# Down products of three late blocks from reduced-precision parts, with two accumulator banks per block

## The chip, the cores and the metric

The kernel runs on one core of a Trainium2 chip. The metric is the device time of one execution in microseconds (us), and the time of the kernel before is the median of three runs. The profile is one execution taken by the hardware profiler; its span runs from the first to the last instruction and is a little shorter than the device time.

## The reference

An attention with polynomial sketches, followed by a SwiGLU feed-forward. Only the second half matters here.

```python
# attention: q, k, v of shape (4, 4, 1088, 32); its output becomes x of shape (4352, 128)
g = x @ w_gate                        # (4352, 1536)
silu = g * (1.0 / (1.0 + np.exp(-g)))
val = x @ w_val                       # (4352, 1536)
return (silu * val @ w_out).astype(np.float32)   # (4352, 128)
```

Inputs are float32, and the products have to come out at about float32 precision.

## The kernel before, in words

All data is held transposed: features on the 128 partitions, tokens along the free dimension. The 1536 hidden features are 12 chunks of 128 (`NCH`), so the weights are `wg[:, j, :]`, `wv[:, j, :]` and `wo[:, j, :]` for chunk j. The tokens of the first batch are three small blocks. Those of the other three batches are seven blocks, the list `line`: six of 480 tokens and a last one of 384. A "unit" is one chunk of one block, and the main loop runs over `y` from 0 to 83, with block `line[y // 12]` and chunk `y % 12`. So units 36 to 47 are the fourth block of the line, 48 to 59 the fifth and 60 to 71 the sixth.

TensorE does a float32 product in two ways. The plain way (one call, two records in the trace) takes float32 operands. The other way cuts each operand into parts of a shorter type, float32r, and gets the same sum from three products. With `w1` the upper part of w, `w0` the rest, `wb` = BETA * w0, `wd` = w1 - BETA * w0, and likewise `x1`, `x0`, `xd` = x1 - BETA * x0, BETA = 4096:

- the "difference product" d = wd . xd is read by ScalarE and scaled by -1/BETA;
- the "sum product" p = w1 . x1 + wb . x0 is read by VectorE, scaled by 1 + 1/BETA and added to it.

The gate and value products of a late unit (`cut_unit` with `both`, from unit 20 on) are made in this way, in this order on each engine:

- TensorE: two difference products (L902), into one pair of PSUM banks, then four part products of the sum (L910, L911), into another pair.
- ScalarE: the copy of the differences, 960 elements wide (L906). Then `finish()` ends the unit before: its Silu (L918).
- VectorE: the combine (L912), 960 wide, from PSUM and the copy.
- GpSimd: hidden = silu * value (L923), also in `finish()`, so one unit later.
- TensorE: `down()`, a plain product (L976) with `wo`, for the hidden chunk of six units before. It accumulates the 12 chunks of a block in one PSUM bank, and after the last one `store` transposes it on VectorE (L1005) and sends it out.

Each engine works through its instructions in the order in which the program issues them; there is no other planner. PSUM has eight banks. In the late units `g2` and `acc` are held for the accumulators of the down products, and the other six are three pairs. `pair()` takes them in turn, and a unit uses two. So the differences of unit y + 2 go where the sums of unit y were, once VectorE has combined them, and the sums of unit y + 1 go where the differences of unit y were, once ScalarE has copied them.

Down products are due when more than five hidden chunks wait, and the loop may issue two in a unit. One line makes the first product of `line[1]` wait a unit longer, as its bank has just been used:

```python
if len(todo) > min(5 + (todo[0] == (line[1], 0)), END - y + 1):
    down()
```

The tokens of the next block are cut into `x1`, `x0`, `xd` nine units before it starts (ScalarE L873, then GpSimd L874) and four units before it (VectorE L878). For the fifth to seventh block of the line that is at the end of units 40 and 44, 51 and 56, 63 and 68. At the start of unit 40 the last group of the attention, `numerators(3)`, also runs.

Of the kernel before, what the change touches and what calls it, by code (L numbers as in the profile page):

```python
# [19 lines left out]
def kernel(  # L20
# [104 lines left out]
    def pair():  # L125

        i = min((i for i in (0, 4, 6) if i not in held), key=lambda i: max(used[i], used[i + 1]))
        touch(i, i + 1)
        return PS[:, i : i + 2, :]
# [13 lines left out]
    wg = const.tile([P, NCH, P], FP32, name="wg")  # L143
    wv = const.tile([P, NCH, P], FP32, name="wv")
    wo = const.tile([P, NCH, D], FP32, name="wo")
    kld = const.tile([P, 4 * NC, Dh], FP32, name="kld")
    qld = const.tile([P, 4 * NC, Dh], FP32, name="qld")
    vld = const.tile([P, H, NC, Dh], FP32, name="vld")
    kT = const.tile([P, NC, 4, 32], FP32, name="kT")
    qT = const.tile([P, 4 * NC, 32], FP32, name="qT")  # L150
    raw = {}
    kpieces = ((0, 5), (5, NC))
    fpieces = ((0, 3), (3, 6), (6, NC))
# [147 lines left out]


    NH = 27
    hbuf = const.tile([P, NH, BW], FP32, name="hbuf")
    slots = [hbuf[:, k, :] for k in range(NH)]
    slot_of = {}

    xT = const.tile([P, NT], FP32, name="xT")
# [297 lines left out]
    def attentions():  # L606

        yield from turn_keys(1)  # L610
        yield from turn_queries(1)
        hold("a")
        kp = wide("a")
        for i, c in enumerate(kpieces):
            key_products(kp[:, i, :], *c)
        ka = apool.tile([P, NC * H, R], FP32, tag="kas", name="kas")

        def sketch(ps, i):
            c0, c1 = kpieces[i]
            return ps[:, i, 0 : 64 * (c1 - c0)].rearrange("p (x t r) -> p x t r", t=2, r=R)  # L620

        for i, (c0, c1) in enumerate(kpieces):
            nc.scalar.copy(ka[:, H * c0 : H * c1, :], sketch(kp, i)[:, :, 0, :])
        phk = apool.tile([P, NC, H, R, R], FP32, tag="phk", name="phk")
        for n, (i, c0, c1) in enumerate(((0, 0, 3), (0, 3, 5), (1, 5, 7), (1, 7, 9))):
            first = H * (c0 - kpieces[i][0])
            kb = sketch(kp, i)[:, first : first + H * (c1 - c0), 1, :]
            key_features(phk, (ka[:, H * c0 : H * c1, :], kb), c0, c1)
            if n == 3:
                release("a")  # L630
            if n % 3 != 1:
                yield
        zs, sums = feature_sums(phk)
        for f in sums:
            f()
        yield from turn_keys(2)
        kvz = wide("a")
        values(kvz[:, 0, :], phk, zs)
        kab, kcopies = sketched(wide("b"), key_products, 2, "kab2")
        fold(kvz[:, 0, :])  # L640
        spread = spread_out(1, kvz[:, 0, :])
        hold("a", "b")
        yield
        qab, copies = sketched(wide("a"), query_sketches, 3, "qab")
        run_copies(copies, 2)
        yield
        run_copies(kcopies, 2)
        release("a", "b")
        for n, _ in enumerate(query_step(1, qab)):
            if n % 2 == 1:  # L650
                yield
        yield
        yield
        numerators(1, spread)
        yield "first"

        phk = apool.tile([P, NC, H, R, R], FP32, tag="phk", name="phk")
        yield from features(phk, kab)
        zs, sums = feature_sums(phk)
        for f in sums:  # L660
            f()
        yield from turn_keys(3)
        yield from turn_queries(2)
        for b in (2, 3):
            yield "pe"
            if b == 3:
                numerators(2, spread)
            hold("a")
            kv = bank()
            kv_bank = [max(used, key=used.get)]  # L670
            release("a")
            values(kv, phk, zs)
            if b == 2:
                kab, copies = sketched(wide("a"), key_products, 2, "kab2")
                run_copies(copies, 2)
            fold(kv)
            spread = spread_out(b, kv)
            touch(*kv_bank)
            yield
            yield "pe"  # L680
            qab, copies = sketched(wide("b"), query_sketches, 3, "qab")
            run_copies(copies, 2)
            yield
            if b == 2:
                yield from turn_queries(3)
                phk = hbuf[:, NH - 6 :, :].rearrange("p s (n h i j) -> p (s n) h i j", h=1, i=R, j=R)
                phk = phk.rearrange("p (c h) o i j -> p c (h o) i j", h=H)
                yield from features(phk, kab)
                zs, sums = feature_sums(phk)
            yield from beside(query_step(b, qab), sums)  # L690
        yield "pe"
        numerators(3, spread)
        yield
# [171 lines left out]
    def cut_tokens(i, engine=nc.gpsimd):  # L865
# [14 lines left out]
            op0=ALU.mult, op1=ALU.add,  # L880
        )

    room = [None, 2]

    def doubles(k):
# [4 lines left out]
        room[1] += k  # L890
        return room[0][:, at : at + k, :]

    def cut_unit(i, j, both=False):

        t0, n = blocks[i]
        x1, x0, xd = (x[:, 0:n] for x in x_parts[i])
        ws = (wg, wv) if both else (wv,)
        parts = [[x[:, j % 3, :] for x in w_parts[id(w), j // 3]] for w in ws]
        ds = pair()[:, :, 0:n] if both else bank()[:, 0:n].unsqueeze(1)
        g = None if both else bank()[:, 0:n]  # L900
        for k, (_, _, wd) in enumerate(parts):
            nc.tensor.matmul(ds[:, k], wd, xd, start=True, stop=True)  # L902
        if not both:
            nc.tensor.matmul(g, wg[:, j, :], xT[:, t0 : t0 + n], start=True, stop=True)  # L904
        sums = doubles(len(ws))[:, :, 0:n]
        nc.scalar.activation(sums, ds, AF.Copy, scale=-1.0 / BETA)  # L906
        finish()
        ps = pair()[:, :, 0:n] if both else bank()[:, 0:n].unsqueeze(1)
        for k, (w1, wb, _) in enumerate(parts):
            nc.tensor.matmul(ps[:, k], w1, x1, start=True, stop=False)  # L910
            nc.tensor.matmul(ps[:, k], wb, x0, start=False, stop=True)  # L911
        nc.vector.scalar_tensor_tensor(  # L912
            out=sums, in0=ps, scalar=1.0 + 1.0 / BETA, in1=sums, op0=ALU.mult, op1=ALU.add
        )

        def last():
            sg = fpool.tile([P, WB], FP32, tag="sg", name="sg", bufs=5)[:, 0:n]
            nc.scalar.activation(sg, sums[:, 0] if both else g, AF.Silu)  # L918
            slot_of[i, j] = slots.pop(0)
            hj = slot_of[i, j]  # L920
            hidden[i, j] = hj
            todo.append((i, j))
            nc.gpsimd.tensor_tensor(out=hj[:, 0:n], in0=sg, in1=sums[:, len(ws) - 1], op=ALU.mult)  # L923

        if both:
            ending.append(last)
        else:
            last()
# [4 lines left out]
    def finish():  # L933
        while ending:
            ending.pop(0)()
# [29 lines left out]
        o, sg = lates.pop(0)  # L965
        nc.gpsimd.tensor_tensor(out=o, in0=o, in1=sg, op=ALU.mult)

    line = list(range(HEAD, len(blocks)))

    def down():  # L970

        i, j = todo.pop(0)
        n = SPLIT if i == LAST else blocks[i][1]
        if j == 0:
            acc[i] = bank("g1" if i == 1 else "g2" if i in line[2::2] else "acc")
        nc.tensor.matmul(  # L976
            acc[i][:, 0:n],
            wo[:, j, :],
            hidden[i, j][:, 0:n],
            start=(j == 0),  # L980
            stop=(j == NCH - 1),
        )
        if i != LAST:
            hidden.pop((i, j))
            slots.append(slot_of[i, j])
        if j == NCH - 1:
            store(i, n)

    def straight(ps, j):

# [238 lines left out]
    run(x_steps or cut_tokens(HEAD, nc.vector))  # L1229

    flat = hbuf[:].rearrange("p s w -> p (s w)")
    slots[:] = [flat[:, WB * k : WB * k + WB] for k in range((NH - 10) * BW // WB)]

# [7 lines left out]
            token_steps.setdefault(at, []).append(gen)  # L1243
    oldest[0] = True
    hold("acc")
    lows = [hbuf[:, NH - 10 + c, :].rearrange("p (c f) -> p c f", f=P) for c in range(4)]
    gate_rows = []
    for y in range(END):
        i, j = line[y // NCH], y % NCH
        if y in GROUPS:  # L1250
            group()
        if y == GATES:
            hold("g2")
        if y == END - 1:
            finish()
            unit(i, j)
        else:
            cut_unit(i, j, both=y >= GATES)
        for _ in range(2):

            if len(todo) > min(5 + (todo[0] == (line[1], 0)), END - y + 1):
                down()
        parts_of(y < GATES or y % 2 == 0)
        if y == 0:
            gate_rows = cut_weights(wg, lows, nc.vector)
        for n, row in enumerate(gate_rows):
            if y >= (0, 2, 6, 6)[n]:
                take(row, 1)
        for gen in token_steps.get(y, ()):
            next(gen, None)  # L1270
    ps = wide("a")[:, 0, 0:D]
    for j in range(NCH):
        if todo and j % 4 == 0:
# [40 lines left out]
```

## Time and profile before

| | us |
|---|---|
| device time, median of 3 (287.96 to 288.39) | 288.08 |
| span of the profile | 286.6 |
| TensorE busy, products | 278.4 |
| VectorE busy | 202.7 |
| ScalarE busy | 165.7 |
| GpSimd busy | 156.2 |

In the lines of the profile, PE is TensorE (PEld its weight loads), DVE VectorE, ACT ScalarE, POOL GpSimd. A row of a group has line, engine, operation, names out<-in with their shapes, count, then busy us, mean ns of one, and the idle time of the engine just before it with what ended that. A product's own time is longer than the distance between two starts, as products are pipelined; distances between starts say what TensorE spends on one. The granted clock of TensorE was 1.00 throughout.

### The profile page before, as it was taken

The page shows a single profiled execution, that of the slowest core. Times are in us where ns is not written, and L with a number is a line of the kernel's source. Part 1 is how long each engine was busy: PE and PEld are TensorE (multiplying, and loading weights), DVE is VectorE, ACT ScalarE, POOL GpSimd, SP SyncE. Part 2 cuts the span into 40 slices and gives each one's busy share as a digit, 9 for nine tenths or more (in the row PEclk, how much of TensorE's full clock was granted, in tenths as well). Part 3 has the DMA queues.
Part 4 walks back from the last instruction along what each step waited for, and adds up shares of the span by engine and source line. Part 5 has one row for each costly group of instructions (what it writes and reads, how often), then busy time and mean ns, then how long its engine had stood idle before and what let it go on. Part 6 is the DMA issues. An engine that isn't in the chain of part 4 may idle for free.

```text
span 286.6 us, 5490 instructions
## 1 busy us (share of the span) xinstructions
PE 278.4 (97%) x2117; PEld 188.7 (66%) x2117; DVE 202.7 (71%) x309; ACT 165.7 (58%) x297; POOL 156.2 (55%) x157
## 2 busy tenths in 40 slices
PE   7899999999999999999999999999999999999994
PEld 6545565666665675555676767757767777677884
DVE  3997988975595977999658889646656655675641
ACT  3468665723401857555276776756776767766750
POOL 3315432279500895499745756546657557566560
PEclk9999999999999999999999999999999999999999
DMA  6574193222311133001000020002000100200201
GB/s 194 154 223 110 55 287 115 80 78 80 98 25 27 26 90 82 2 0 27 11 16 0 1 37 0 0 2 34 0 0 15 23 0 0 34 0 2 34 1 28
DMA packets 26137, 14.27 MB, mean 50 GB/s; under 512 B 19840, under 2 KB 24192, under 8 KB 26112
## 3 DMA queue, kind: packets, MB, share of 16 engines
q1 hardware_dynamic: 25456, 13.84, 18.8%
q8 instruction: 16, 0.26, 0.4%
q10 hardware_dynamic: 656, 0.10, 0.2%
q14 instruction: 9, 0.07, 0.1%
HBM read 11.41 MB, written 2.23 MB: 48 GB/s over the span
## 4 chain that ended last, share of the span: by engine, by line
PE 89%; DVE 5%; ACT 2%; DMA 2%; issue 1%; SPq 0%; DVEq 0%; ACTq 0%
PE PS L976 28%; PE PS L945 16%; PE PS L902 11%; PE PS L910 10%; PE PS L911 10%; PE PS L904 5%; PE PS L774 2%; PE PS L333 2%; PE PS L345 2%; DMA kld<-in_k_dram 2%; PE PS L379 1%; DVE sum L912 1%; PE PS L991 1%; PE PS L488 1%; PE PS L436 1%
## 5 line engine op out<-in xcount | busy, mean ns | idle before, releaser
L923 POOL TENSOR_TENSOR hbuf<-sg,sum 128x480 f32<-128x480 f32 (+1 forms) x83 | 103.3, 1249 | 60.2 <-ACT sg L918 52.9
L912 DVE SCALAR_TENSOR_TENSOR sum<-PS,sum 128x960 f32<-128x960 f32 (+2 forms) x83 | 83.5, 1006 | 48.3 <-ACT sum L906 42.5
L906 ACT ACTIVATE sum<-PS 128x960 f32<-128x960 f32 (+2 forms) x83 | 70.9, 854 | 51.0 <-PE PS L902 50.9
L976 PE MATMUL PS<-hbuf,wo 128*128 128x480 f32 (+3 forms) x240 | 100.3, 517 | 0.0
L976 PEld LDWEIGHTS PS<-hbuf,wo 128*128 128x128 f32 x240 | 45.0, 189 | 13.1 <-issue 0.9
L902 PE MATMUL PS<-xd,gphq 128*128 128x480 f32 (+1 forms) x63 | 44.8, 711 | 0.5 <-DVE xd L878 0.5
L910 PE MATMUL PS<-x,w 128*128 128x480 f32 (+1 forms) x83 | 38.6, 465 | 0.0
L918 ACT ACTIVATE sg<-sum 128x480 f32<-128x480 f32 (+1 forms) x63 | 36.5, 580 | 0.6 <-DVE sum L912 0.6
L902 PE MATMUL PS<-xd,wd 128*128 128x480 f32 (+1 forms) x83 | 35.8, 431 | 0.5 <-DVE xd L878 0.5
L911 PE MATMUL PS<-x,wb 128*128 128x480 f32 (+1 forms) x83 | 31.3, 378 | 0.0
L945 PE MATMUL PS<-xT,wg 128*128 128x384 f32 (+1 forms) x74 | 29.5, 480 | 0.0
L945 PE MATMUL PS<-xT,wv 128*128 128x384 f32 (+1 forms) x74 | 28.8, 471 | 0.2 <-DVE wv L279 0.2
L949 ACT ACTIVATE sg<-PS 128x384 f32<-128x384 f32 (+1 forms) x31 | 14.4, 467 | 21.3 <-PE PS L945 19.6
L902 PEld LDWEIGHTS PS<-xd,wd 128*128 128x128 f32 x83 | 15.7, 189 | 15.5 <-issue 14.6
L910 PE MATMUL PS<-x,graw 128*128 128x480 f32 (+1 forms) x63 | 23.6, 374 | 0.2 <-ACT xT L791 0.2
L960 DVE TENSOR_TENSOR hbuf<-sg,PS 128x384 f32<-128x384 f32 (+1 forms) x31 | 16.2, 525 | 10.5 <-PE PS L945 10.1
L911 PE MATMUL PS<-x,graw 128*128 128x480 f32 (+1 forms) x63 | 23.4, 371 | 0.0
L902 PEld LDWEIGHTS PS<-xd,gphq 128*128 128x128 f32 x63 | 11.8, 188 | 13.7 <-issue 11.1
L945 PEld LDWEIGHTS PS<-xT,wv 128*128 128x128 f32 x74 | 13.8, 190 | 9.2 <-DVE hbuf L960 0.9
L910 PEld LDWEIGHTS PS<-x,w 128*128 128x128 f32 x83 | 15.6, 188 | 5.9 <-issue 3.4
L945 PEld LDWEIGHTS PS<-xT,wg 128*128 128x128 f32 x74 | 13.3, 189 | 9.3 <-issue 1.2
L911 PEld LDWEIGHTS PS<-x,wb 128*128 128x128 f32 x83 | 15.6, 188 | 5.8 <-issue 4.3
(131 smaller groups left out, 345.8 us busy)
## 6 DMA issues: line engine op xcount, KB each, us to landing
kld<-in_k_dram SPq DMA_DIRECT2D x4, 544.0 KB, 4.4
vld<-in_v_dram SPq DMA_DIRECT2D x12, 144.0 KB, 4.4
qld<-in_q_dram SPq DMA_DIRECT2D x3, 544.0 KB, 3.5
raw<-in_moe_w_out_dram SPq DMA_DIRECT2D x4, 384.0 KB, 3.8
raw<-in_moe_w_gate_dram SPq DMA_DIRECT2D x3, 384.0 KB, 3.7
raw<-in_moe_w_val_dram SPq DMA_DIRECT2D x3, 384.0 KB, 3.7
out_dram<-o SPq DMA_DIRECT2D x16, 60.0 KB, 2.0
vld<-in_v_dram SPq DMA_DIRECT2D x4, 112.0 KB, 4.4
```

Source lines behind the costliest of these rows:

```text
L902: nc.tensor.matmul(ds[:, k], wd, xd, start=True, stop=True)
L904: nc.tensor.matmul(g, wg[:, j, :], xT[:, t0 : t0 + n], start=True, stop=True)
L906: nc.scalar.activation(sums, ds, AF.Copy, scale=-1.0 / BETA)
L910: nc.tensor.matmul(ps[:, k], w1, x1, start=True, stop=False)
L911: nc.tensor.matmul(ps[:, k], wb, x0, start=False, stop=True)
L912: nc.vector.scalar_tensor_tensor(out=sums, in0=ps, scalar=1.0 + 1.0 / BETA, in1=sums, op0=ALU.mult, op1=ALU.add)
L918: nc.scalar.activation(sg, sums[:, 0] if both else g, AF.Silu)
L923: nc.gpsimd.tensor_tensor(out=hj[:, 0:n], in0=sg, in1=sums[:, len(ws) - 1], op=ALU.mult)
L945: nc.tensor.matmul(o[:, 0:n], w[:, j, :], xT[:, t0 : t0 + n], start=True, stop=True)
L949: nc.scalar.activation(sg[:, 0:n], g[:, 0:n], AF.Silu)
L960: nc.vector.tensor_tensor(out=hj[:, 0:n], in0=sg[:, 0:n], in1=u[:, 0:n], op=ALU.mult)
L976: nc.tensor.matmul(acc[i][:, 0:n], wo[:, j, :], hidden[i, j][:, 0:n], start=(j == 0), stop=(j == NCH - 1),)
```

## The change

In the fourth, fifth and sixth block of the line (`line[3:6]`) the down products of the six odd chunks are made from parts like the others. That is 18 of 84 down products of the line. It needs:

- `cut_down`: parts of the odd chunks of `wo`, made once in nine steps at units 24, 26, ... 40. The even chunks are scaled by -BETA, so that their plain products can go into the differences' bank.
- `cut_hidden`: parts of each odd hidden chunk of unit y: `h1` on ScalarE in unit y + 2 behind the Silu, `h0` on GpSimd in unit y + 3 ahead of that unit's product, `hd` on VectorE in unit y + 4 ahead of that unit's combine.
- two banks per block: `g2` takes the difference products and the scaled plain ones, `acc` the sum products. Before, blocks took `g2` and `acc` in turn.
- `put_together`: in the unit behind a block's last down product ScalarE copies `g2` (behind the Silu), in the next VectorE adds `acc` (`sum2`, ahead of the combine), and in the one after that `store` runs.
- the first down product of the fifth to seventh block waits one unit longer, so one unit has none and the next has two.
- storage: the parts take the place of tiles that are no longer read (`late`, `kld`, `qld`, `vld`, `kT`, `qT`).

```diff
+    DOWN = [(i, j) for i in line[3:6] for j in range(1, NCH, 2)]
+    def cut_down():
+        n = NCH // 2
+        parts = const.tile([P, 3, n, D], F32R, tag="late", name="dparts", bufs=1)
+        w1, wb, wd = (parts[:, k] for k in range(3))
...
+        odd, even = wo[:, 1::2, :], wo[:, 0::2, :]
+        cs = [slice(c, c + 2) for c in range(0, NCH // 2, 2)]
+        nc.scalar.activation(w1, odd, AF.Copy, scale=CUT)
+        yield
+        for c, x in zip(cs, low):
+            nc.gpsimd.tensor_tensor(
+                out=x, in0=odd[:, c], in1=whole(w1[:, c]), op=ALU.subtract
+            )
+            yield
+        for c, x in zip(cs, low):
+            nc.scalar.activation(wb[:, c], x, AF.Copy, scale=BETA)
+        yield
+        for c in cs:
+            nc.gpsimd.tensor_tensor(
+                out=wd[:, c], in0=whole(w1[:, c]), in1=whole(wb[:, c]), op=ALU.subtract
+            )
+            yield
+        nc.scalar.activation(scaled, even, AF.Copy, scale=-BETA)
+    def cut_hidden(y, i, j):
...
+        h_sets.append(h_sets.pop(0))
+        h1, h0, hd = h_parts[i, j] = [x[:, 0:n] for x in h_sets[-1]]
+        h = hidden[i, j][:, 0:n]
+        add_to(behind, y + 2, lambda: nc.scalar.activation(h1, h, AF.Copy, scale=CUT))
+        add_to(before, y + 3, lambda: nc.gpsimd.tensor_tensor(
+            out=h0, in0=h, in1=whole(h1), op=ALU.subtract
+        ))
+        add_to(before, y + 4, lambda: nc.vector.scalar_tensor_tensor(
+            out=hd, in0=whole(h0), scalar=-BETA, in1=whole(h1), op0=ALU.mult, op1=ALU.add
+        ))
@@ cut_unit @@
         nc.scalar.activation(sums, ds, AF.Copy, scale=-1.0 / BETA)
+        now(before, y)
         finish()
+        now(behind, y)
@@ down @@
-            acc[i] = bank("g1" if i == 1 else "g2" if i in line[2::2] else "acc")
+            acc[i] = bank("g1" if i == 1 else "g2" if i in line[2:] else "acc")
+        mine = [c for c in range(NCH) if (i, c) in DOWN]
+        if mine and j == mine[0]:
+            acc[i, "p"] = bank("acc")
+        sides = dict(start=(j == 0), stop=(j == NCH - 1))
+        if j in mine:
+            w1, wb, wd = [down_parts[x][:, j // 2, :] for x in ("w1", "wb", "wd")]
+            h1, h0, hd = h_parts.pop((i, j))
+            nc.tensor.matmul(acc[i][:, 0:n], wd, hd, **sides)
+            p = acc[i, "p"][:, 0:n]
+            nc.tensor.matmul(p, w1, h1, start=(j == mine[0]), stop=False)
+            nc.tensor.matmul(p, wb, h0, start=False, stop=(j == mine[-1]))
+        else:
+            w = down_parts["scaled"][:, j // 2, :] if mine else wo[:, j, :]
+            nc.tensor.matmul(acc[i][:, 0:n], w, hidden[i, j][:, 0:n], **sides)
...
+    def put_together(y, i, n):
...
+        add_to(behind, y + 1, lambda: nc.scalar.activation(s, d, AF.Copy, scale=-1.0 / BETA))
+        add_to(before, y + 2, lambda: nc.vector.scalar_tensor_tensor(
+            out=s, in0=p, scalar=1.0 + 1.0 / BETA, in1=s, op0=ALU.mult, op1=ALU.add
+        ))
+        add_to(before, y + 3, lambda: store(i, n))
@@ main loop @@
-            if len(todo) > min(5 + (todo[0] == (line[1], 0)), END - y + 1):
-                down()
+            wait = todo[0][1] == 0 and todo[0][0] in line[1:2] + line[4:]
+            if len(todo) > min(5 + wait, END - y + 1):
+                down(y)
...
+        if y in range(24, 42, 2):
+            next(down_steps, None)
```

More of the change, by code (lines that the diff above doesn't have):

```diff
@@ L145 @@
     wo = const.tile([P, NCH, D], FP32, name="wo")
[L146 to L150, printed above, removed]
+    kld = const.tile([P, 4 * NC, Dh], FP32, tag="kld", name="kld", bufs=1)
+    qld = const.tile([P, 4 * NC, Dh], FP32, tag="qld", name="qld", bufs=1)
+    vld = const.tile([P, H, NC, Dh], FP32, tag="vld", name="vld", bufs=1)
+    kT = const.tile([P, NC, 4, 32], FP32, tag="kT", name="kT", bufs=1)
+    qT = const.tile([P, 4 * NC, 32], FP32, tag="qT", name="qT", bufs=1)
     raw = {}
@@ L303 @@
     NH = 27
-    hbuf = const.tile([P, NH, BW], FP32, name="hbuf")
-    slots = [hbuf[:, k, :] for k in range(NH)]
+    NL = 10
+    hbuf = const.tile([P, NH - NL, BW], FP32, name="hbuf")
+    late = const.tile([P, NL, BW], FP32, tag="late", name="late", bufs=1)
+    slots = [(hbuf[:, k, :] if k < NH - NL else late[:, k - NH + NL, :]) for k in range(NH)]
     slot_of = {}
@@ L685, in attentions @@
                 yield from turn_queries(3)
-                phk = hbuf[:, NH - 6 :, :].rearrange("p s (n h i j) -> p (s n) h i j", h=1, i=R, j=R)
+                phk = late[:, NL - 6 :, :].rearrange("p s (n h i j) -> p (s n) h i j", h=1, i=R, j=R)
                 phk = phk.rearrange("p (c h) o i j -> p c (h o) i j", h=H)
@@ L881, in cut_tokens, with add_to, now @@
         )
+    line = list(range(HEAD, len(blocks)))
+    DOWN = [(i, j) for i in line[3:6] for j in range(1, NCH, 2)]
+    down_parts = {}
+    h_parts = {}
+    h_sets = []
+    before, behind = {}, {}
+    def add_to(where, y, f):
+        where.setdefault(y, []).append(f)
+    def now(where, y):
+        for f in where.pop(y, ()):
+            f()
+    def cut_down():
+        n = NCH // 2
+        parts = const.tile([P, 3, n, D], F32R, tag="late", name="dparts", bufs=1)
+        w1, wb, wd = (parts[:, k] for k in range(3))
+        scaled = apool.tile([P, n, D], FP32, tag="zs", name="scaled")[:]
+        low = [apool.tile([P, 2, D], FP32, tag=tag, name="low" + tag)[:] for tag in ("kas", "dot", "kab2")]
+        down_parts.update(w1=w1, wb=wb, wd=wd, scaled=scaled)
+        odd, even = wo[:, 1::2, :], wo[:, 0::2, :]
[16 more added lines that the diff above has]
+        nc.scalar.activation(scaled, even, AF.Copy, scale=-BETA)
@@ new lines, in cut_hidden @@
+    def cut_hidden(y, i, j):
+        if not h_sets:
+            x = []
+            for tag in ("kld", "qld", "vld", "kT", "qT"):
+                t = const.tile([P, 2, WB], F32R, tag=tag, name="h" + tag, bufs=1)
+                x += [t[:, k, :] for k in range(2)]
+            h_sets.extend(x[k : k + 3] for k in range(0, 9, 3))
+        n = blocks[i][1]
+        h_sets.append(h_sets.pop(0))
[8 more added lines that the diff above has]
+        ))
@@ L891, in doubles, with cut_unit @@
         return room[0][:, at : at + k, :]
-    def cut_unit(i, j, both=False):
+    def cut_unit(i, j, both=False, y=None):
         t0, n = blocks[i]
@@ L923, in last @@
             nc.gpsimd.tensor_tensor(out=hj[:, 0:n], in0=sg, in1=sums[:, len(ws) - 1], op=ALU.mult)
+            if (i, j) in DOWN:
+                cut_hidden(y, i, j)
         if both:
@@ L966, in catch_up, with down @@
         nc.gpsimd.tensor_tensor(out=o, in0=o, in1=sg, op=ALU.mult)
-    line = list(range(HEAD, len(blocks)))
-    def down():
+    def down(y=None):
         i, j = todo.pop(0)
@@ L974, in down @@
         if j == 0:
-            acc[i] = bank("g1" if i == 1 else "g2" if i in line[2::2] else "acc")
[L976 to L982, printed above, removed]
+            acc[i] = bank("g1" if i == 1 else "g2" if i in line[2:] else "acc")
[13 more added lines that the diff above has]
+            nc.tensor.matmul(acc[i][:, 0:n], w, hidden[i, j][:, 0:n], **sides)
         if i != LAST:
@@ L986, in down @@
         if j == NCH - 1:
-            store(i, n)
+            if mine:
+                put_together(y, i, n)
+            else:
+                store(i, n)
+    def put_together(y, i, n):
+        s = fpool.tile([P, WB], FP32, tag="sg", name="sum2", bufs=5)[:, 0:n]
+        d, p = acc.pop(i)[:, 0:n], acc.pop((i, "p"))[:, 0:n]
+        acc[i] = s
+        add_to(behind, y + 1, lambda: nc.scalar.activation(s, d, AF.Copy, scale=-1.0 / BETA))
[3 more added lines that the diff above has]
+        add_to(before, y + 3, lambda: store(i, n))
     def straight(ps, j):
@@ L1231 @@
     flat = hbuf[:].rearrange("p s w -> p (s w)")
-    slots[:] = [flat[:, WB * k : WB * k + WB] for k in range((NH - 10) * BW // WB)]
+    slots[:] = [flat[:, WB * k : WB * k + WB] for k in range((NH - NL) * BW // WB)]
     END = len(line) * NCH
@@ L1245 @@
     hold("acc")
-    lows = [hbuf[:, NH - 10 + c, :].rearrange("p (c f) -> p c f", f=P) for c in range(4)]
+    lows = [late[:, c, :].rearrange("p (c f) -> p c f", f=P) for c in range(4)]
     gate_rows = []
+    down_steps = cut_down()
     for y in range(END):
@@ L1257 @@
         else:
-            cut_unit(i, j, both=y >= GATES)
+            cut_unit(i, j, both=y >= GATES, y=y)
         for _ in range(2):
-            if len(todo) > min(5 + (todo[0] == (line[1], 0)), END - y + 1):
-                down()
+            wait = todo[0][1] == 0 and todo[0][0] in line[1:2] + line[4:]
+            if len(todo) > min(5 + wait, END - y + 1):
+                down(y)
         parts_of(y < GATES or y % 2 == 0)
```

## The prediction

> **What bounds the kernel now.** I read the page first: busy shares, then the chain, then the costliest groups. TensorE is busy 97% and carries 89% of the chain; VectorE, the next engine of the chain, has 5%.
>
> ```profile
> PE 278.4 (97%) x2117; PEld 188.7 (66%) x2117; DVE 202.7 (71%) x309; ACT 165.7 (58%) x297; POOL 156.2 (55%) x157
> ...
> PE 89%; DVE 5%; ACT 2%; DMA 2%; issue 1%; SPq 0%; DVEq 0%; ACTq 0%
> ...
> L923 POOL TENSOR_TENSOR hbuf<-sg,sum 128x480 f32<-128x480 f32 (+1 forms) x83 | 103.3, 1249 | 60.2 <-ACT sg L918 52.9
> L912 DVE SCALAR_TENSOR_TENSOR sum<-PS,sum 128x960 f32<-128x960 f32 (+2 forms) x83 | 83.5, 1006 | 48.3 <-ACT sum L906 42.5
> L906 ACT ACTIVATE sum<-PS 128x960 f32<-128x960 f32 (+2 forms) x83 | 70.9, 854 | 51.0 <-PE PS L902 50.9
> L976 PE MATMUL PS<-hbuf,wo 128*128 128x480 f32 (+3 forms) x240 | 100.3, 517 | 0.0
> ```
>
> These shares average different stages, so next the stretch that the change touches, by windows (us busy, instructions, for PE, PEld, DVE, ACT, POOL):
>
> ```profile
> 196.00:256.00 60.00, 60.00 (x229) 42.78 (x228) 37.08 (x34) 42.20 (x59) 37.24 (x31) 1.00 0.08 12
> ```
>
> The last two numbers are DMA; transfers play no part. TensorE has no gap here, and the other three are at 62 to 70%. The timeline shows one unit (start, duration):
>
> ```profile
> 222.47 0.97 PE L976 MATMUL PS<-hbuf,wo 128*128 128x480 f32 x2
> 222.90 0.75 PE L902 MATMUL PS<-xd,gphq 128*128 128x480 f32 x1
> 223.39 1.23 POOL L923 TENSOR_TENSOR hbuf<-sg,sum 128x480 f32<-128x480 f32 x1 [0.90 <-ACT sg L918]
> 223.50 0.38 PE L902 MATMUL PS<-xd,wd 128*128 128x480 f32 x1
> 223.72 0.38 PE L910 MATMUL PS<-x,graw 128*128 128x480 f32 x1
> 223.94 0.38 PE L911 MATMUL PS<-x,graw 128*128 128x480 f32 x1
> 223.97 0.97 ACT L906 ACTIVATE sum<-PS 128x960 f32<-128x960 f32 x1 [0.66 <-PE PS L902]
> 224.60 0.97 PE L976 MATMUL PS<-hbuf,wo 128*128 128x480 f32 x2
> 224.84 0.59 ACT L918 ACTIVATE sg<-sum 128x480 f32<-128x480 f32 x1
> 224.98 1.16 DVE L912 SCALAR_TENSOR_TENSOR sum<-PS,sum 128x960 f32<-128x960 f32 x1 [0.97 <-ACT sum L906]
> 225.51 1.23 POOL L923 TENSOR_TENSOR hbuf<-sg,sum 128x480 f32<-128x480 f32 x1 [0.90 <-ACT sg L918]
> 226.05 1.20 DVE L878 SCALAR_TENSOR_TENSOR xd<-x,x 128x480 fp32r<-128x480 f32 x1
> ```
>
> The unit repeats every 224.60 - 222.47 = 2.13 us. Part products start 0.217 apart (223.50, 223.72, 223.94), so six take 1.30 and the plain down product the remaining 0.83. Counted from R(y), the true start of unit y's first part product (223.28 here): ScalarE's copy runs from 0.69 to 1.66, VectorE's combine from 1.70 to 2.86, and in the next unit Silu ends at 2.15 and GpSimd's product runs from 2.23 to 3.46. Back to back, the starts lie closer than the durations: copy 0.87, Silu 0.50, combine 1.07, GpSimd 1.19.
>
> **What the Trainium skill says.** "SBUF — State Buffer", section "SBUF: two separate sides": VectorE and GpSimd share a port pair, an exclusive lock held for a whole instruction; a VectorE operation with two SBUF inputs blocks a GpSimd one that reads SBUF, and the reverse. The trace agrees:
>
> ```profile
> 173.37 0.62 DVE L878 SCALAR_TENSOR_TENSOR xd<-x,x 128x480 fp32r<-128x480 f32 x1
> ```
>
> With GpSimd idle this operation takes 0.62. At 226.05 it took 1.20: GpSimd's product ran until 226.74, and it ended 0.51 later. "PSUM — Partial Sum Buffer", section "Engine vs sequencer instructions": the queues of ScalarE, VectorE and GpSimd are strict FIFO; nothing in the trace passes a waiting instruction. "TensorE: Matmul & The Clock Gate", section "Back-to-back issue gap", gives N/2.4 + 2.5 ns, 202.5 for N = 480; the trace has 217, which I use. No page prices a plain fp32 product; the 0.83 is the trace's.
>
> **Part by part.**
> *TensorE.* 18 plain products become 3 part products each: 0.83 - 3 x 0.217 = 0.18 saved, 18 x 0.18 = **3.24 us**, all on the path.
>
> *Weight parts (units 24 to 40).* Two ScalarE operations of 768 elements (0.81, the row of 768), three of 256 (about 0.37), six GpSimd ones of 256 (0.73, the row of 256). They lie beside TensorE: ScalarE has 2.13 - 1.37 = 0.76 free per unit, GpSimd 0.94. Nothing, except that the last 768 meets a token cut at unit 40.
>
> *Hidden parts.* Per pair of units: one ScalarE operation (0.59; 0.50 back to back, as L873), one GpSimd subtraction (1.21; 1.17, as L874), one VectorE one (0.62 if the lock is free, 1.20 if not, as L878). A pair is now 2 x 2.13 - 0.18 = 4.08. ScalarE needs 2 x 1.37 + 0.50 = 3.24 and VectorE 2 x 1.07 + 0.6 to 1.13, at most 3.27. GpSimd needs 2 x 1.19 + 1.17 = 3.55, and it is locked out about 0.52 more: 4.07 of 4.08. **GpSimd is full**, where it was at 62%. In step it fits exactly: one gap of 0.53 per pair, as long as the VectorE operation. What adds GpSimd work makes it late, and three engines queue behind: h1 (ScalarE) waits for GpSimd's product, with the next copy behind it; hd (VectorE) waits for h0, with the next combine behind it; the combine frees the PSUM pair that TensorE refills two units later.
>
> *Turn of a block.* This happens twice the same way, after units 53 and 65. The first product of the new block is put off by a unit: unit 54 has none (1.30 long), 55 has two. Both accumulators, g2 and acc, are single, so the new block waits until ScalarE has read g2 and VectorE's sum2 has read acc. A token cut sits at 51 and 63. From R(51) = 0, unhindered: R(53) = 4.08, R(55) = 7.33. ScalarE: h1(49) ends 2.65, the token copy 3.15. GpSimd: product(50) to 3.46, token subtraction to 4.6, h0(49) to 5.8, product(51) 5.75 to 6.95. VectorE: hd(49) is ready at 5.85, but GpSimd has just begun: blocked to 6.95, done 7.5; combine(53) behind it ends 8.6 instead of 6.94 + 0.1. TensorE may start unit 55 at 8.65: **1.3 us of wait**. On: product(52) to 8.7, h0(51) to 9.85, product(53) to 11.0; hd(51) blocked until 11.0, done 11.55; sum2 (0.64, as L912 at 480) behind it ends 12.1. TensorE reaches the first product into acc at 8.65 + 1.30 + 0.83 + 0.22 = 11.0 and starts it at 12.2: **1.2 us more**. So 2.5 per turn, 5.0 for two. Bounds: without lock and lateness, hd(51) ends 3.97 and sum2 4.55 after R(54), and TensorE comes at 3.65, 0.97 wait; with GpSimd 0.4 late at the start, 2.9.
>
> *Entry.* The first differences use g2 right behind the block before it, with no put-off. The transpose (0.67, L1005) reads g2 behind hd(37) and combine(41); it ends about 3.7 after R(41), where TensorE arrives at 3.43: 0.3. With ScalarE 0.6 late from the token copy and the 768 operation at unit 40, 0.7. I take 0.5.
>
> *Last turn (unit 78).* No token cut and no hidden parts: ScalarE's read of g2 ends about 0.25 after TensorE wants it, and the short unit 78 costs 0.08: 0.3.
>
> *Nothing:* the store's transpose (it was there before, and stays in VectorE's idle time), 3 ScalarE and 3 VectorE operations of the putting together apart from the waits above, the even weights' scaling (same product, other operand).
>
> Sum: -3.24 + 5.0 + 0.5 + 0.3 = +2.56, so 288.08 + 2.56 = **290.6 us**.
>
> **Rivals.**
> *A, the saving stands (other side).* Waits hidden by the five-unit distance from product to down product. For: no engine alone exceeds TensorE in a pair. Against: the PSUM pair allows two units, not five. With 0.8 of waits left: 288.08 - 3.24 + 0.8 = 285.6.
> *B, bank waits alone.* The token cut's lateness is swallowed and hd finds the lock free half the time: 1.2 per turn, 0.3 entry, 0.2 last: -3.24 + 2.9 = -0.34, 287.7. For: VectorE's turn depends on who asks first. Against: GpSimd's slack.
> *C, GpSimd is the bound throughout.* Hidden parts run from unit 40 to 74: 35 products x 1.19, 18 + 3 subtractions x 1.17, 21 lockouts x 0.52 = 77.1 us in a stretch that takes TensorE 35 x 2.13 - 3.24 = 71.3; plus about 1 of starvation at each turn, less 1.5 that lateness may carry over and 0.8 of slack at the end: (77.1 - 71.3) + 2.0 - 2.3 = 5.5 of waits, plus 0.8 for entry and last turn and about 1 if ScalarE's queue adds its own: +4.1, 292.2.
>
> **How the numbers follow.** Main case 0.53, A 0.13, B 0.20, C 0.14. Faster: A, and a third of B: 0.19. Same: half of B: 0.10. The rest is slower: 0.71. The range, 286.9 to 292.3, leaves out most of A (0.11) and the upper part of C (0.08); its width is the wait per turn, 0.97 to 2.9, twice.
>
> **What would show it.** Right: part products of the down chunks 0.217 apart; GpSimd above 90% busy in units 40 to 74; L878-like hd operations of about 1.2; TensorE gaps of about 1.3 before a unit's first product near unit 55 and 67, released by VectorE's combine, and of about 1.2 before the first product into acc, released by sum2. Wrong: no TensorE gap over 0.5 at the turns (A), gaps only before acc (B), gaps in every pair (C).

## The result, and the profile after

The changed kernel takes 290.78 us (290.69 to 291.17) against 288.07 us: a ratio of 1.0095, 95% interval 1.0077 to 1.0112. It is slower by 2.7 us, and 0.2 us from the forecast of 290.6.

Line numbers move with the change: the combine L912 is now L979, the copy of the differences L971, GpSimd's product L990, the difference products L967, the plain down product L1057. The products of the down parts are L1051 (difference), L1053 and L1054 (sum), `h0` is L941, `hd` L944, `sum2` L1073. The page of the changed kernel, in the places shown of before:

```profile
PE 277.9 (96%) x2135; PEld 191.6 (66%) x2135; DVE 228.3 (79%) x330; ACT 178.5 (62%) x323; POOL 186.7 (65%) x181
...
PE 83%; DVE 6%; POOL 4%; issue 2%; ACT 2%; DVEq 0%; ACTq 0%
...
L990 POOL TENSOR_TENSOR hbuf<-sg,sum 128x480 f32<-128x480 f32 (+1 forms) x83 | 106.3, 1287 | 32.6 <-ACT sg L985 25.2
L979 DVE SCALAR_TENSOR_TENSOR sum<-PS,sum 128x960 f32<-128x960 f32 (+2 forms) x83 | 82.9, 1003 | 22.9 <-ACT sum L971 16.8
...
L967 PE MATMUL PS<-xd,gphq 128*128 128x480 f32 (+1 forms) x63 | 36.3, 576 | 2.8 <-DVE sum L979 2.3
```

TensorE still looks busy 96% of the time. What is new is at the ends of the lines: the first difference product of a unit now sat idle 2.8 us, 2.3 of it until a combine ended, and GpSimd has come into the chain with 4%. The windows of the changed kernel show how full the stretch is:

```profile
196.00:218.00 22.00, 22.00 (x94) 17.30 (x93) 19.85 (x17) 19.00 (x28) 20.53 (x17) 1.00 0.07 11
```

GpSimd is busy 20.53 of 22.00, 93%, and VectorE 90%; before, in the longer stretch shown, it was 62% for each. (Time in which an operation is held up by the other engine counts as busy.) Next the wait view of TensorE from 196 to 256, after. It has line, what it waited for, us in total, times, longest:

```profile
PE PS L967 <- DVE sum L979: 2.3, 2, 1.3
PE PS L1053 <- DVE sum L1073: 1.7, 2, 0.8
```

These are the two waits of the prediction, each at two turns: on the combine, and on `sum2` ahead of `acc`. For the kernel before, the same question brings no line at all. The timeline around the first turn, TensorE's part and then VectorE's and GpSimd's:

```profile
219.18 0.37 PE L978 MATMUL PS<-x,graw 128*128 128x480 f32 x1
220.87 0.49 PE L967 MATMUL PS<-xd,gphq 128*128 128x480 f32 x1 [1.32 <-DVE sum L979]
...
222.73 0.76 PE L1051 MATMUL PS<-hqld,dparts 128*128 128x480 f32 x1
224.31 0.49 PE L1053 MATMUL PS<-hkld,dparts 128*128 128x480 f32 x1 [0.82 <-DVE sum L1073]
```

```profile
218.08 1.67 DVE L944 SCALAR_TENSOR_TENSOR hqld<-hkld 128x480 fp32r<-128x480 f32 x1 [0.82 <-POOL hkld L941]
219.67 2.25 DVE L979 SCALAR_TENSOR_TENSOR sum<-PS,sum 128x960 f32<-128x960 f32 x2
222.04 1.65 DVE L944 SCALAR_TENSOR_TENSOR hvld<-hvld,hqld 128x480 fp32r<-128x480 f32 x1
223.61 0.64 DVE L1073 SCALAR_TENSOR_TENSOR sum<-PS,sum 128x480 f32<-128x480 f32 x1
```

```profile
215.64 1.22 POOL L876 TENSOR_TENSOR x<-xT,x 128x480 fp32r<-128x480 f32 x1
216.83 1.22 POOL L941 TENSOR_TENSOR hkld<-hbuf,hkld 128x480 fp32r<-128x480 f32 x1
218.01 2.80 POOL L990 TENSOR_TENSOR hbuf<-sg,sum 128x480 f32<-128x480 f32 x2
```

Read from the bottom: the token subtraction (L876) pushes `h0` of unit 49 to 218.05. GpSimd starts its next product at 218.01, just before VectorE begins `hd` at 218.08, and `hd` takes 1.67 in place of the 0.62 that this kind of operation took beside an idle GpSimd. The two combines run behind it from 219.67 on, and TensorE starts unit 55 at 220.87, 1.47 after the last product of unit 54 was through (219.18 + 0.217). Then `hd` of unit 51 is held up again, until 223.69, `sum2` ends at 224.25, and the first product into `acc` starts at 224.31.

To add up waits I use one marker, the start of the second difference product of each unit, and its distance from that of the unit before. A wait shows in it some 0.25 longer than the idle time in brackets, which is counted from a modelled end (1.58 and 1.32 at unit 55). From unit 42 to 82 the changed kernel loses 2.81 us on the one before: -2.87 saved on 18 chunks (0.16 each), 0.30 at unit 43 (entry), 2.65 at units 55 and 56, 2.37 at 67 and 68, 0.36 at 79 and 80 (last turn).

### The profile page after: what moved, and what is told of

The parts are those of the page before. It is cut to its first block, busy times and chain, and to the rows that moved or that the text cites. A ratio compares the mean times of both kernels' runs of the same rounds, so it can differ in the third digit from the quotient of the medians.

```text
span 288.8 us, 5616 instructions
## 1 busy us (share of the span) xinstructions
PE 277.9 (96%) x2135; PEld 191.6 (66%) x2135; DVE 228.3 (79%) x330; ACT 178.5 (62%) x323; POOL 186.7 (65%) x181
## 4 chain that ended last, share of the span: by engine, by line
PE 83%; DVE 6%; POOL 4%; issue 2%; ACT 2%; DVEq 0%; ACTq 0%
PE PS L1057 21%; PE PS L1014 16%; PE PS L967 10%; PE PS L977 9%; PE PS L978 9%; PE PS L969 5%; PE PS L776 2%; POOL hbuf L990 2%; PE PS L234 2%; PE PS L335 2%; PE PS L347 1%; PE PS L1053 1%; PE PS L1054 1%; PE PS L381 1%; DVE sum L979 1%
## 5 line engine op out<-in xcount | busy, mean ns | idle before, releaser
L990 POOL TENSOR_TENSOR hbuf<-sg,sum 128x480 f32<-128x480 f32 (+1 forms) x83 | 106.3, 1287 | 32.6 <-ACT sg L985 25.2
L979 DVE SCALAR_TENSOR_TENSOR sum<-PS,sum 128x960 f32<-128x960 f32 (+2 forms) x83 | 82.9, 1003 | 22.9 <-ACT sum L971 16.8
L971 ACT ACTIVATE sum<-PS 128x960 f32<-128x960 f32 (+2 forms) x83 | 70.8, 853 | 38.4 <-PE PS L967 36.7
L1057 PE MATMUL PS<-hbuf,wo 128*128 128x480 f32 (+3 forms) x142 | 57.5, 506 | 0.0
L967 PE MATMUL PS<-xd,gphq 128*128 128x480 f32 (+1 forms) x63 | 36.3, 576 | 2.8 <-DVE sum L979 2.3
L967 PE MATMUL PS<-xd,wd 128*128 128x480 f32 (+1 forms) x83 | 35.8, 431 | 0.5 <-DVE xd L880 0.5
L1057 PEld LDWEIGHTS PS<-hbuf,wo 128*128 128x128 f32 x142 | 26.5, 189 | 8.7 <-issue 0.9
L967 PEld LDWEIGHTS PS<-xd,wd 128*128 128x128 f32 x83 | 15.7, 189 | 10.9 <-issue 9.3
L967 PEld LDWEIGHTS PS<-xd,gphq 128*128 128x128 f32 x63 | 11.8, 188 | 14.2 <-DVE sum L979 6.4
L969 PE MATMUL PS<-xT,wg 128*128 128x480 f32 x40 | 19.3, 564 | 0.0
```

The costliest lines, as they stand in the source:

```text
L979: nc.vector.scalar_tensor_tensor(out=sums, in0=ps, scalar=1.0 + 1.0 / BETA, in1=sums, op0=ALU.mult, op1=ALU.add)
L1057: nc.tensor.matmul(acc[i][:, 0:n], w, hidden[i, j][:, 0:n], **sides)
```

## The experiments

The distances of that marker in us, for the kernels whose traces are compared below. The unit is the later of the two. Without a wait, 55 is 1.30 and 56 is 2.78 wherever the put-off and the parts are in place. The columns: before; the change; then the experiments by their main edit.

| unit | before | change | token earlier | sum2 first | load only | turn only | token on VectorE | both edits | and copy first | hd once behind |
|---|---|---|---|---|---|---|---|---|---|---|
| 43 | 2.11 | 2.41 | 2.41 | 2.40 | 2.11 | 2.41 | 2.42 | 2.40 | 2.40 | 2.41 |
| 53 | 2.13 | 2.11 | 2.97 | 2.11 | 2.13 | 2.12 | 2.12 | 2.11 | 2.12 | 2.12 |
| 55 | 2.13 | 2.88 | 1.98 | 2.90 | 2.34 | 1.31 | 2.16 | 2.15 | 2.15 | 1.29 |
| 56 | 2.13 | 3.87 | 3.90 | 2.78 | 2.12 | 3.14 | 3.88 | 2.78 | 2.77 | 3.12 |
| 59 | 2.13 | 2.12 | 2.12 | 2.12 | 2.13 | 2.12 | 2.12 | 2.12 | 2.11 | 3.25 |
| 67 | 2.11 | 2.54 | 2.01 | 2.57 | 2.20 | 1.29 | 1.90 | 1.90 | 1.89 | 1.28 |
| 68 | 2.10 | 3.88 | 3.89 | 2.75 | 2.12 | 3.15 | 3.88 | 2.76 | 2.75 | 2.97 |
| 80 | 1.48 | 2.27 | 2.27 | 2.27 | 1.48 | 2.33 | 2.26 | 2.26 | 2.10 | 2.10 |

**The load alone.** Parts made, but not used.

```diff
-        mine = [c for c in range(NCH) if (i, c) in DOWN]
+        mine = []
-            wait = todo[0][1] == 0 and todo[0][0] in line[1:2] + line[4:]
+            wait = todo[0] == (line[1], 0)
```

> All the work that makes parts on ScalarE, GpSimd and VectorE stays, but the down products are the plain ones of the kernel before, one bank per block, no put-off and no putting together. The parts are made and not read. Theory (the load fits beside TensorE except where the short unit and the bank reads take the slack away): 288.1 to 289.0, no wait over 0.5. Rival C (GpSimd is the bound): the load alone costs 3 to 5.5 us, 291 to 293.5.

Measured 288.17 us, ratio to before 0.9993 (0.9979 to 1.0006). In the windows of this run GpSimd is the fullest beside TensorE:

```profile
196.00:256.00 60.00, 60.00 (x228) 42.34 (x227) 55.04 (x48) 49.65 (x73) 56.20 (x45) 1.00 0.08 13
```

So 94% of GpSimd and 92% of VectorE cost nothing by themselves, with the token cuts in their places. Only 0.2 shows at unit 55 and 0.1 at 67. A pair of units is 4.23 here, and no unit is short. That GpSimd bounds the whole stretch (rival C) is out.

**The turn alone.** Two banks, put-off and putting together, all products plain. (`sum2` then takes `acc` times 1, and the group in `g2` ends with chunk 10.)

```diff
-            nc.tensor.matmul(acc[i][:, 0:n], wd, hd, **sides)
-            nc.tensor.matmul(p, w1, h1, start=(j == mine[0]), stop=False)
-            nc.tensor.matmul(p, wb, h0, start=False, stop=(j == mine[-1]))
+            nc.tensor.matmul(p, wo[:, j, :], hidden[i, j][:, 0:n], start=(j == mine[0]), stop=(j == mine[-1]))
...
-            if (i, j) in DOWN:
-                cut_hidden(y, i, j)
```

> The bank scheme alone: even chunks into g2, odd ones into acc, put-off and putting together as in the change, but all 84 down products plain and no hidden parts made (sum2 adds acc times 1, as acc holds plain products of the odd chunks). Theory (the turn is cheap when no hd stands ahead of sum2 and GpSimd is not late): 0.3 for the entry, 0.4 for the last turn, at most 0.3 for each of the other two: 288.5 to 289.3. Rival B (single banks cost 1.2 a turn by themselves): 290.5 to 291.

Measured 289.01 us, ratio 1.0027 (1.0009 to 1.0044). The entry costs 0.30, the last turn 0.4, the other two 0.2 each (units 55 and 56 together 4.45, against 4.26 before). So at a turn the single banks by themselves cost a sixth of the 1.2 that rival B gave them. Load and turn cost 0 and 0.7 apart; together they cost the whole saving and 2.7 more.

**sum2 ahead of hd.** One operation changes its place on VectorE.

```diff
-        add_to(before, y + 2, lambda: nc.vector.scalar_tensor_tensor(
+        before.setdefault(y + 2, []).insert(0, lambda: nc.vector.scalar_tensor_tensor(
             out=s, in0=p, scalar=1.0 + 1.0 / BETA, in1=s, op0=ALU.mult, op1=ALU.add
```

> In units 55 and 67 (and 79) VectorE does sum2 ahead of hd instead of behind it. Theory (sum2 is late only because hd, which waits for GpSimd, stands ahead of it on VectorE): the wait ahead of the first product into acc, 0.96 each time, goes to zero; hd and the combine behind it come 0.6 later, of which up to 0.3 may come back at unit 57: 288.9 to 289.4. Rival (all waits are one lateness of GpSimd, which only shows at acc): the same wait appears one or two units later, 290.8.

Measured 288.73 us, ratio to before 1.0020 (1.0007 to 1.0032), 2.05 less than the change. The wait ahead of `acc` is gone at both turns: unit 56 falls from 3.87 to 2.78, unit 68 from 3.88 to 2.75, and nothing comes back later. VectorE in this run:

```profile
221.89 0.66 DVE L1073 SCALAR_TENSOR_TENSOR sum<-PS,sum 128x480 f32<-128x480 f32 x1
222.47 1.17 DVE L944 SCALAR_TENSOR_TENSOR hvld<-hvld,hqld 128x480 fp32r<-128x480 f32 x1
223.56 1.14 DVE L979 SCALAR_TENSOR_TENSOR sum<-PS,sum 128x960 f32<-128x960 f32 x1
```

`sum2` is done before TensorE gets there. The wait was one of order, not of work.

**Token cut earlier.**

```diff
-        for at in {2: (20, 22), 4: (40, 44)}.get(m, (NCH * m - 9, NCH * m - 4)):
+        for at in {2: (20, 22), 4: (40, 44), 5: (48, 56), 6: (60, 68)}.get(m, (NCH * m - 9, NCH * m - 4)):
```

> Token cuts of the last two blocks at units 48 and 60 instead of 51 and 63, nothing else. Theory (GpSimd is late at the turn because the token subtraction falls three units ahead of the short unit, and works lateness off slowly, 4.07 of 4.08 us per pair being taken): the wait ahead of unit 55 and 67 shrinks from about 1.4 to between 0.3 and 1.0, the wait ahead of acc stays at about 0.9: 289.0 to 290.0. Rival B (only the single banks count): no difference, 290.8. Rival C (GpSimd is the bound throughout): the waits move to units 50 to 53, and the time stays at 290.8.

Measured 290.62 us (ratio to before 1.0097, 1.0071 to 1.0124): no gain, as rival C had it here, though the load alone speaks against its cause. The wait is split, 0.86 at unit 53 and 0.68 at 55, together 1.54 against the 1.58 of the change. With three units more to work it off, GpSimd starts the product behind `h0` of unit 49 at 218.00, where it was 218.01: by the trace's time it is as late as it was.

**Token subtraction on VectorE.**

```diff
-        gen = cut_tokens(i)
+        gen = cut_tokens(i, nc.vector if m in (5, 6) else nc.gpsimd)
```

> The token subtraction at units 51 and 63 goes from GpSimd to VectorE, at the same place in the program; nothing else. Theory (GpSimd is full in these blocks, so the token subtraction's 1.2 us has to come out as a wait of TensorE, wherever it is put): the waits ahead of unit 55 and 67, 1.6 and 1.3 us, fall to 0.4 or less, the waits ahead of acc stay: 288.0 to 288.9. Rival (the first wait comes from the short unit and VectorE's hd alone, whatever GpSimd has to do): no difference or slower, as VectorE has more to do: 290.8 to 291.5.

Measured 289.47 us, ratio to before 1.0042 (1.0027 to 1.0057), above the 288.0 to 288.9 expected. The wait at unit 55 falls from 1.58 to 0.86, at 67 from 1.24 to 0.6. That is not the whole worth of the token subtraction, as GpSimd did not get its 1.2 us back: on VectorE the subtraction held up `h0`, which took 1.67 in place of 1.22.

```profile
215.71 0.64 DVE L876 TENSOR_TENSOR x<-xT,x 128x480 fp32r<-128x480 f32 x1
215.76 1.67 POOL L941 TENSOR_TENSOR hkld<-hbuf,hkld 128x480 fp32r<-128x480 f32 x1
217.40 2.81 POOL L990 TENSOR_TENSOR hbuf<-sg,sum 128x480 f32<-128x480 f32 x2
```

The wait follows the start of that next product on GpSimd. Counted from the marker of units 53 and 65 it starts at 1.66 and 1.31 in the change and at 0.93 and 0.66 here; the waits are 1.58 and 1.24, 0.86 and 0.60, each some 0.07 less. One pair earlier, ahead of the token subtraction, the same start in the change is at 0.58 and 0.35. So an estimate from these figures is that 0.5 and 0.3 of wait would be left with no token subtraction in the way.

**Both edits, and the copy of g2 ahead of the Silu.** The third edit puts `put_together`'s ScalarE operation into `before` in place of `behind`.

> Both: the token subtraction at 51 and 63 on VectorE, and sum2 ahead of hd. Theory (two separate causes): both waits of a turn go, what stays is 0.3 for the entry, 0.4 for the last turn and up to 0.5 at each other turn, against a saving of 18 x 0.15: 286.1 to 287.0, faster than the kernel before. Rival (the waits are one lateness that shows at whichever place is left): 288 or more.

> As the run with both, and ScalarE's copy of g2 in the unit behind a block's last down product goes ahead of the Silu instead of behind it. Theory (the last turn waits for ScalarE's read of g2): about 0.3 less than with both alone, all of it in unit 79 to 80. Rival (the last turn's 0.36 comes from the short unit): no difference.

Measured 287.27 us (ratio 0.9973, 0.9962 to 0.9984) and 287.02 us (0.9957, 0.9941 to 0.9974). The two waits are separate: taking both away gives about the sum of what each gave (3.5 against 2.05 and 1.3). Both runs beat the kernel before, the second by 1.2 us. The first missed its forecast (286.1 to 287.0), as 0.85 and 0.6 stay at units 55 and 67. The copy takes 0.17 off the last turn (unit 80, 2.27 to 2.10), not 0.3.

**All h0 on VectorE.**

> All 18 h0 subtractions go from GpSimd to VectorE, token subtractions and order as in the change. Theory (GpSimd's fullness is what makes the token subtraction show): GpSimd has 1.2 us more per pair, the wait ahead of unit 55 and 67 falls to 0.5 or less; VectorE is then the fullest, 3.9 of 4.08, and sum2 stands behind two operations, so the wait ahead of acc stays or grows to 1.5: 288.3 to 290. Rival (the lock, not GpSimd's own time, makes the lateness): the lock now has the same work in it, so no difference, 290.8.

Measured 288.66 us, ratio to before 1.0015 (1.0004 to 1.0027), 2.1 less than the change and within what the theory gave. Its only trace is of an execution of 563.75 us, in which part products start 0.43 apart and TensorE waits for nobody, so where the waits went in the others was not seen.

**hd behind the combine.** First alone, then with the token subtraction on VectorE and the early copy of g2.

```diff
-        add_to(before, y + 4, lambda: nc.vector.scalar_tensor_tensor(
+        add_to(combined, y + 4, lambda: nc.vector.scalar_tensor_tensor(
             out=hd, in0=whole(h0), scalar=-BETA, in1=whole(h1), op0=ALU.mult, op1=ALU.add
...
+        now(combined, y)   # directly behind the combine
```

> hd goes behind the combine of its unit on VectorE instead of ahead of it, so that the combine (and sum2) no longer wait for GpSimd; all else as in the change, token subtraction on GpSimd too. hd is due at the down product two units later. Theory (TensorE waits because combine and sum2 stand behind hd on VectorE): the wait ahead of acc goes to zero; of the wait ahead of unit 55 and 67 the part through VectorE goes, and the part through ScalarE (h1 waits for GpSimd's product, with the copy behind it) stays, up to 0.9: 287.2 to 288.6. Rival (GpSimd's time itself bounds the stretch, so it doesn't matter who stands behind whom): the waits reappear, 290 to 290.8.

> hd behind the combine, token subtractions at 51 and 63 on VectorE, ScalarE's copy of g2 ahead of the Silu. Theory: of the waits only the entry's 0.3, the last turn's 0.2 and about 0.2 at each other turn stay, against 18 x 0.15 = 2.7 saved: 286.1 to 286.7, the fastest of all. Rival: GpSimd's fullness leaves the 0.85 and 0.6 of the run with both edits and the early copy: 287.0.

Measured 289.88 us (1.0057, 1.0038 to 1.0076) and 289.29 us (1.0037, 1.0024 to 1.0050): both misses. TensorE's waits in the first of them, from 186 on:

```profile
PE PS L977 <- ACT sum L971: 2.0, 2, 1.1
PE PS L1058 <- DVE o L1095: 1.2, 1, 1.2
```

The waits on the combine and on `sum2` are gone, as expected. But `hd` of unit 37, which before filled idle time ahead of the combine, now runs between the combine and the transpose that frees `g2` at the entry. The transpose starts at 195.32 in place of 194.08, and unit 43 costs 1.4 in place of 0.30. That was overlooked. And ScalarE's copy is late instead, as it stands behind `h1`, which waits for GpSimd. In the second run the wait on the combine is back, a unit earlier: 0.87 at unit 54 and 0.70 at 66. There the token subtraction on VectorE took 1.67, with the combine of unit 52 behind it.

**hd behind the combine in units 53 and 65 alone**, with the three edits of the fastest run.

> As the run with all three edits that was fastest (token subtraction on VectorE, sum2 first, copy of g2 ahead of the Silu), and hd goes behind the combine in units 53 and 65 alone, just ahead of the short unit; elsewhere it stays ahead, so the entry is as in that run. Theory (what is left at the turns, 0.85 and 0.58, is the combine of unit 53 behind hd, which waits for GpSimd's port): both fall to 0.2 or less: 285.8 to 286.4, against 287.02. Rival (ScalarE's h1, which waits for GpSimd's product, is next in line): 286.5 to 287.

Measured 287.74 us, ratio 0.9981 (0.9973 to 0.9989), above both forecasts and 0.7 slower than the fastest. Unit 55 is free of waits (1.29), so `hd` ahead of the combine was what stayed there. But 0.34 appears at unit 56, 1.13 at unit 59, and 0.2 at each of 68, 73 and 75. In the fastest run VectorE is already this full:

```profile
196.00:256.00 60.00, 59.08 (x248) 45.90 (x247) 57.81 (x53) 51.14 (x76) 55.20 (x44) 1.00 0.08 13
```

At 57.81 of 60.00 there is little place left to put an operation off to. But about 13 of the 57.81 are no work of its own: they are what 20 operations, the `hd` and token ones, last beyond the 0.64 that they take alone. Whether they can be placed where GpSimd leaves them alone, or work taken away from either engine, was not tried.

**Without the put-off.** `wait` as it was in the kernel before.

> The first down product of the fifth to seventh block is not put off: unit 54 issues it and has to wait for ScalarE's copy of g2; all else as in the change. Theory (the put-off trades one wait for another, the lateness of hd and of sum2 is the cause): the wait ahead of unit 55 moves to g2 in unit 54 (about 1.3), the wait ahead of acc stays at about 0.9: 290.2 to 291.3. Rival (the short unit is the cause): the first wait goes, 288.2 to 289.

Measured 293.17 us, ratio 1.0169 (1.0146 to 1.0193): slower than either theory said. The short unit isn't the cause; without it TensorE waits 2.4, 2.15 and 1.1 at the three turns for ScalarE's copy of `g2`, which stands behind the Silu, the combine and, at the first two, `hd`. The wait ahead of `acc` is gone, which neither theory said. So the put-off is worth having, at the last turn too, where the change loses only 0.36.

## Why the prediction was right, step by step

- *The saving* was put at 0.18 per chunk, 3.24. It was 0.16, 2.87: the plain product takes 0.81 to 0.83 along the stretch, and I had the upper end.
- *Weight parts, hidden parts beside TensorE:* nothing inside the blocks. Shown by the load alone (288.17), whose pairs are 0.15 longer, and by the units inside the blocks of the change (2.12 at unit 59), which show no wait.
- *GpSimd full:* 93% in the stretch ahead of the first turn, but 88% from 196 to 256, where TensorE's waits leave it idle: the sign of 90% throughout did not come. And the load alone shows that 94% costs nothing by itself. The sharper sign is the earlier token cut, which changed nothing.
- *The turn*, 2.5 each: 2.65 and 2.37. The working holds step by step. From R(51), 212.05 in the trace, `hd` of unit 49 is done at 7.70 (7.5 forecast), unit 55 starts at 8.82 (8.65), `sum2` ends at 12.20 (12.1) and the first product into `acc` starts at 12.26 (12.2). The two terms came out at 1.58 and 1.09 for the first turn (1.3 and 1.2 forecast). The second term is shown to be `sum2` behind `hd`, by the reorder. That the first goes through `hd` ahead of the combine is shown by putting `hd` behind it in that unit. What the working had too small is what stays without the token subtraction: it allowed the combine 0.1 of lateness, where the estimate above leaves a wait of 0.5 and 0.3.
- *Entry* 0.5: 0.30. *Last turn* 0.3: 0.36. Shown by the turn alone, which has both (0.30 and 0.4).
- *The sign of hd* was mis-sized. I wrote that such operations would take about 1.2; two of three groups have a median of about 1.66, as in my own working of the turn (ready at 5.85, done at 7.5):

```profile
L944 DVE SCALAR_TENSOR_TENSOR hqld<-hkld x6: 871/1668/1672, 191.8 to 258.4; 128x480 fp32r<-128x480 f32 x6
L944 DVE SCALAR_TENSOR_TENSOR hvld<-hvld,hqld x6: 1611/1655/1671, 196.2 to 262.4; 128x480 fp32r<-128x480 f32 x6
L944 DVE SCALAR_TENSOR_TENSOR hqT<-hkT x6: 644/1048/1666, 202.0 to 266.2; 128x480 fp32r<-128x480 f32 x6
```

Where GpSimd has its next product ready it starts it as `h0` ends (218.01 and 218.05 above), so `hd`, which waits for `h0`, meets it just begun. So it was for 14 of the 18, which took 1.45 or more.

- *The sum.* The saving came 0.37 short and the entry 0.2 cheap, which partly cancel, and the two turns miss by 0.15 and -0.13. That the total is only 0.2 off is in part luck.

Rival A's five-unit distance did not help: the waits sit on the PSUM pairs and on `acc`, not on the hidden chunks.

## What to carry to other kernels

In this kernel, work shifted from TensorE to other engines was free only while their queues stayed in step. Look at what stands behind each new operation in its queue, and keep anything that frees a PSUM bank ahead of anything that waits for another engine: here one such reorder was worth 2.05 of the 2.7 lost. But see what the operation moved back then stands ahead of: the same thought applied to `hd` gave misses. And test load and order apart: the load cost nothing, the bank scheme 0.7, and only together did they lose more than the saving.

## What was not expected of the hardware

TensorE's granted clock halved in a gap of 2.56 us. In the run without the put-off the last product before the wait was through at 219.58 and the next started at 222.14. The windows of that run, granted clock third from the end:

```profile
219.00:222.00 3.00, 0.73 (x4) 0.30 (x2) 3.00 (x3) 2.43 (x4) 3.00 (x3) 0.95 0.00 0
222.00:225.00 3.00, 2.86 (x5) 1.79 (x6) 2.30 (x3) 0.09 (x1) 1.33 (x2) 0.50 0.00 0
225.00:228.00 3.00, 3.00 (x14) 2.49 (x14) 1.74 (x2) 2.84 (x5) 1.45 (x2) 0.98 0.02 5
```

By an estimate from these figures, about 3 us at 0.50 cost some 1.4 more. The other executions bear it out: the traced one and one more had a mean granted clock of 0.994 and took 293.75 and 293.84 us, the other two had 0.998 and 1.000 and took 292.24 and 292.59. So the same program lost the clock in some executions only, and even without the loss it is slower than forecast. The gap at the second turn of the same trace, 2.32 us counted the same way (248.01 to 250.33), left the clock alone. The Trainium skill, "TensorE: Matmul & The Clock Gate", section "What's actually happening", states that the half rate comes after an idle window of about 3.4 us, and that the window runs free. Here a shorter gap did it in the traced execution and a nearly equal one did not; that the window's place decides would fit this, but no run here shows it.
